# Weight loads of a fused delta-rule attention and MLP kernel, each split by partitions into two or four pieces

## The chip, the cores and the metric

The kernel runs on one core of a Trainium2 chip. A core has five engines that run side by side, each with a queue of its own that it works off in order: PE (TensorE: matmuls, and the weight loads before them, shown as PEld), DVE (VectorE), ACT (ScalarE), POOL (GpSimd) and SP (SyncE, which here only issues transfers). Transfers between the off-chip memory and the on-chip memory (SBUF, 128 partitions) are carried by 16 DMA engines. The metric is the time of the program in device microseconds (us), the median of several runs.

## The reference

For 4 batches and 8 heads a linear attention with the delta rule runs over 768 steps; its outputs, put side by side over the heads, give 3072 tokens of 384 numbers, which go through an MLP with 2048 hidden units.

```python
# q, k, v: (4, 8, 768, 48); beta: (4, 8, 768)
k_n = k / (np.linalg.norm(k, axis=-1, keepdims=True) + 1e-06)
for t in range(S):
    kt, vt, bt = (k_n[:, :, t].copy(), v[:, :, t].copy(), beta[:, :, t, None].copy())
    y[:, :, t] = np.einsum('bhd,bhde->bhe', q[:, :, t], state)
    v_old = np.einsum('bhde,bhd->bhe', state, kt)
    state = state + bt[:, :, :, None] * np.einsum('bhd,bhe->bhde', kt, vt - v_old)
# x: (3072, 384) from y; w_in: (384, 2048); w_out: (2048, 384)
h = x @ w_in
g = 0.5 * h * (1.0 + np.tanh(c * (h + 0.044715 * h * h * h)))
return g @ w_out
```

All inputs and the output are float32.

## The kernel before

**Tiling.** The 768 steps are cut into 12 chunks of 64 (`NC`), and each chunk into two units (`u = 2 * c + x`), each with half of the heads. For a unit, `prep` loads and normalizes k, turns k and q so that the head dimension lies on partitions (`kT`), takes the products of all pairs of steps (`G`, line 614), masks them (`ln`, `wp`) and inverts a triangular matrix by five rounds of doubling (operations `A` and `B`, line 684, with the block-diagonal tile `bd`). Then `chain` carries the state through the chunk: `K` and `R` (lines 729 and 742, where `R` subtracts from the scaled v), `U` (lines 755 and 765), `S` for the next state, `O` for the output. The output of a chunk is turned (`xT`) and fed to `mlp`: the up projection (`up`, line 842) with `W1`, the activation (`gelu`, line 847), the down projection (`down`, line 854) with `W2`, and the store of the rows. A chunk's MLP is 16 up blocks of three matmuls and, for each of two halves of its rows, 16 down matmuls in four operations of four.

**Weights.** `W1` is [128, 3, 2048] and `W2` is [128, 16, 384], both bf16 in SBUF, while `moe_w_in` and `moe_w_out` are float32 in memory: the transfer casts. Each is loaded in two halves by the function `weights` (lines 516 to 526), issued from POOL: the halves of `W1` by hidden units 0 to 1023 and 1024 to 2047, those of `W2` by the hidden blocks 0 to 7 and 8 to 15. Each load has 128 partitions. An up block waits for its half of `W1`, a down operation for its half of `W2`:

```python
A("pe", z + "up", up, reads=xn + [f"W1{0 if i < FC // 2 else 1}"], ...
A("pe", z + "down", down, reads=[f"{gn}.{f}" for f in range(i, i + 4)] + [f"{gn}s{i}", f"W2{0 if i < FC // 2 else 1}"], ...
```

**Order.** Every engine's order is written out by hand in the table `ORDER`, by names such as `w1.-3/0` (operation `w1` with position -3, first of its kind). `Flow.plans` works out the waits from what each operation reads and writes; several transfers that write the same buffer with the same semaphore (`dma=`) count it up together, and a reader waits for all of them. On POOL the four loads stand among other work: `w1.-3/0` between two `X1` selects (line 674), `w1.-2.9/0` between the halves of `R0` (line 734), `w2.-2/0` after `triw.1/0` (line 459) and before `binv.6/0` (line 550) and `vb.2.5/0` (line 739, the scaling of v that `R` waits for), and `w2.-1.9/0` between the `X1` selects of units 4 and 5. PE's queue begins with matmuls on zeros (`fill`, line 471) between the real work. PE's accumulators (PSUM) are given out by `BANKS` in PE's order, so a matmul can also wait for a bank that another engine has yet to read.

Of the kernel before, what the change touches and what calls it, by code (L numbers as in the profile page):

```python
# [122 lines left out]
    "pool": """  # L123
        masks.-12/0 masks.-12/2 bdz.4/0 half.-28/0 masks.-12/1 ident.-29/0 tmplz.-11/0 two.-12/0 ident2.-29/0 mlo.-12/0 two.-12/1
        bdz.7/0 mup.-12/0 mup.-12/1 mlo.-12/1 bdz.5/0 bneg.-28/0 X1h.0/0 X1h.0/1 binv.-140/0 X1h.1/1 kn.2/0 X1h.1/0 kn.3/0 X1.2/0
        X1.3/0 X1.2/1 w1.-3/0 X1.3/1 sq.6/0 binv.4/0 triw.-1/0 sq.8/0 R0.0.5/1 kn.4/0 w1.-2.9/0 R0.0.5/0 qb.4.01/0 pow.6/0 eps.6/0
        kn.5/0 triw.1/0 w2.-2/0 binv.6/0 vb.2.5/0 bdz.2/0 X1.4/1 X1.4/0 w2.-1.9/0 X1.5/0 X1.5/1 pow.8/0 kn.7/0 qb.6.01/0 eps.8/0
        qb.7.01/0 vb.4.5/0 kn.6/0 binv.8/0 kn.9/0 kn.8/0 bdz.3/0 qb.8.01/0 qb.9.01/0 pow.10/0 X1.6/0 eps.10/0 X1.6/1 X1.7/1 X1.7/0
        binv.10/0 X1.8/0 X1.8/1 X1.9/0 X1.9/1 kn.11/0 sq.12/0 vb.6.5/0 kn.10/0 qb.10.01/0 qb.11.01/0 bdc.8/1 bdc.8/0 pow.12/0
        bdc.9/1 X1.10/1 bdc.9/0 eps.12/0 X1.10/0 qb.13.01/0 binv.12/0 sq.14/0 X1.11/0 X1.11/1 qb.12.01/0 bdc.8/3 bdc.8/2 kn.13/0  # L130
# [215 lines left out]
def bass_deltanet__then__act_gelu_tanh_kernel(  # L346
# [10 lines left out]
    DM, FF = moe_w_in.shape  # L357
    assert (B, H, D) == (4, 8, 48) and DM == H * D and S % C == 0 and FF % 512 == 0
    NC, FC, J = S // C, FF // 128, DM // 128
# [4 lines left out]
    LIVE = {i: slice(0, C - 16) if i == 4 else slice(32, C) if i == 5 else slice(0, C) for i in range(1, 6)}  # L364
    UNIT = {4: slice(C - 16, C), 5: slice(0, 32)}

    F = Flow()
    A = F.add

    with nc.allow_non_contiguous_dma("strided loads"), nc.allow_low_precision("bf16 pipeline"):  # L370
        def sb(name, shape, dt=BF16, n=1):
            t = [nc.alloc_sbuf_tensor(f"{name}{i}", shape, dt).ap() for i in range(n)]
            return t if n > 1 else t[0]
# [17 lines left out]
        sq = sb("sq", [128, 2 * H, D], F32, 2)  # L391
# [19 lines left out]
        W1 = sb("W1", [128, J, FF])  # L411
        W2 = sb("W2", [128, FC, DM])
# [56 lines left out]
        def warm_up(n):  # L469
            def fill(e, P, i):  # L470
                return e.matmul(P(f"fill{i}")[:, :], wz[:, 0:128], wz[:, 0:512])  # L471
            for i in range(n):
                A("pe", "fill", lambda e, P, i=i: fill(e, P, i), reads=["wz"], alloc=(f"fill{i}", 1), frees=[f"fill{i}"], mode="m", pos=1e6, mm=1)
# [42 lines left out]
        def weights():  # L516
            w1v = moe_w_in.rearrange("(j p) f -> p j f", p=128)
            w2v = moe_w_out.rearrange("(n p) e -> p n e", p=128)
            for i in range(2):
                f0 = FF // 2 * i  # L520
                A("pool", "w1", lambda e, P, f0=f0: e.dma_start(W1[:, :, f0:f0 + FF // 2], w1v[:, :, f0:f0 + FF // 2]),
                  writes=[f"W1{i}"], dma=f"w1{i}", pos=-3 + 0.1 * i)
            for i in range(2):
                n0 = FC // 2 * i
                A("pool", "w2", lambda e, P, n0=n0: e.dma_start(W2[:, n0:n0 + FC // 2, :], w2v[:, n0:n0 + FC // 2, :]),
                  writes=[f"W2{i}"], dma=f"w2{i}", pos=-2 + 0.1 * i)

        def norms(c):
            z, r = "" if c else "0", c % NR
# [419 lines left out]
        for c in range(3):  # L949
            norms(c)  # L950
        weights()
        A("act", "tabG", lambda e, P: e.activation(one[:, :], one[:, :], ACT.Gelu_apprx_tanh),
          reads=["nrm00", "nrm01", "nrm10", "nrm20"], writes=["one"], pos=3)
# [17 lines left out]
        warm_up(ORDER["pe"].count("fill/"))  # L971
        F.schedule(ORDER, BANKS)
        G = Flow()
        banks = general(G)
        G.in_turn(banks)
        F.emit(nc, psum, G, flag[0:1, 0:1], flagged)

# [27 lines left out]
```

## Time and profile before

| | us |
|---|---|
| median of 3 runs (252.04 to 254.88) | 253.32 |
| the profiled execution | 252.5 |
| its span, first to last instruction | 250.8 |
| PE busy | 239.4 |
| DVE busy | 192.9 |
| ACT busy | 175.8 |
| POOL busy | 151.9 |

The profile shows one execution. Busy time is the time in which an engine ran something; an engine in order that waits for a semaphore holds up everything behind it in its queue. The granted clock is that of PE, as a share of full speed; over the whole span it was 0.993. The share of DMA is the mean busy share of the 16 DMA engines (it can exceed 1, because packets overlap), and GB/s is what they moved (counted in written bytes: the four weight loads together are 3.15 MB in the queue that carries them).

### The profile page before, as it was taken

To read this page: it belongs to the slowest core of one execution; us is meant where nothing else is said; L and a number is where in the kernel's file an instruction comes from. 1 tells how busy PE (TensorE), PEld (TensorE's weight loads), DVE (VectorE), ACT (ScalarE), POOL (GpSimd) and SP (SyncE) were. 2 spreads that over 40 slices of the span, in tenths; PEclk is the share of its full clock that TensorE was granted. 3 is DMA by queue.
4 is the path that set the end of the run, shared out by engine and by line. 5 is a ranking of instruction groups with operands and counts; after the bars stand their busy time and mean duration, and the time that the engine had idled before them with its cause. 6 is when DMAs were issued, how large, how long until landed. Compare 5 with 4: busy or idle time off the path is not lost.

```text
span 250.8 us, 11724 instructions
## 1 busy us (share of the span) xinstructions
PE 239.4 (95%) x5239; PEld 186.5 (74%) x5239; DVE 192.9 (77%) x330; ACT 175.8 (70%) x282; POOL 151.9 (61%) x229
## 2 busy tenths in 40 slices
PE   7799789799999998999999999999999999999996
PEld 3366577677877986888777898877887788886773
DVE  4999677859999997897898897998798688823110
ACT  5887569686998996886777786666775656663250
POOL 8268874894948667979858886877834444020000
PEclk9999979999999999999999999999999999999999
DMA  7989999974997997987898989948191241300124
GB/s 126 134 167 149 196 188 170 166 126 59 195 141 132 163 160 111 134 149 166 170 103 129 159 110 165 139 79 120 37 164 33 69 90 26 84 1 4 34 63 118
DMA packets 103367, 29.62 MB, mean 118 GB/s; under 512 B 96624, under 2 KB 102512, under 8 KB 103312
## 3 DMA queue, kind: packets, MB, share of 16 engines
q1 hardware_dynamic: 99248, 25.28, 64.5%
q0 software_dynamic: 2880, 3.15, 8.2%
q8 instruction: 43, 0.70, 1.2%
q10 hardware_dynamic: 1184, 0.39, 0.7%
q14 instruction: 12, 0.10, 0.1%
HBM read 20.55 MB, written 4.72 MB: 101 GB/s over the span
## 4 chain that ended last, share of the span: by engine, by line
PE 84%; DVE 5%; DMA 4%; issue 3%; ACT 2%; POOL 1%; ACTq 0%; POOLq 0%
PE ps L854 24%; PE ps L842 23%; PE ps L684 19%; PE ps L471 4%; PE ps L729 3%; PE ps L614 3%; PE ps L656 3%; DMA kT<-tok 2%; DMA xT<-xo 2%; PE ps L765 2%; PE ps L787 1%; PE ps L774 1%; PE ps L594 1%; ACT xi L418 1%; POOL vraw L739 1%
## 5 line engine op out<-in xcount | busy, mean ns | idle before, releaser
L842 PE MATMUL ps<-xT,W 128*128 128x256 bf16 x576 | 78.4, 273 | 0.4 <-DVE rs L742 0.2
L418 ACT ACTIVATE bd<-ps 64x512 bf16<-64x512 f32 x115 | 65.6, 588 | 14.6 <-PE ps L684 13.0
L854 PE MATMUL ps<-W,gT 128*128 128x384 bf16 x384 | 74.6, 326 | 0.0
L847 ACT ACTIVATE gT<-ps 128x1024 bf16<-128x1024 f32 x48 | 48.8, 1022 | 19.0 <-PE ps L842 18.4
L842 PEld LDWEIGHTS ps<-xT,W 128*128 128x128 bf16 x576 | 50.2, 98 | 7.4 <-DVE rs L742 0.4
L691 DVE TENSOR_TENSOR rt<-ps,two 128x512 bf16<-128x512 f32 x66 | 44.5, 685 | 9.9 <-PE ps L684 9.3
L678 POOL COPY bd<-xi 64x256 f32<-64x256 f32 x64 | 25.4, 403 | 34.3 <-ACT xi L418 26.3
L854 PEld LDWEIGHTS ps<-W,gT 128*128 128x128 bf16 x384 | 33.2, 98 | 16.1
L674 POOL TENSOR_SCALAR_AFFINE_SELECT bd<-ln 64x512 bf16<-64x512 bf16 x44 | 28.8, 657 | 18.2 <-DVE ln L635 14.0
L418 DVE CAST bd<-ps 64x512 bf16<-64x512 f32 x41 | 27.4, 680 | 3.9 <-PE ps L684 3.3
L691 DVE TENSOR_TENSOR rl<-ps,two 128x384 bf16<-128x384 f32 (+1 forms) x44 | 21.0, 483 | 12.1 <-PE ps L684 11.6
L418 ACT ACTIVATE xi<-ps 128x512 bf16<-128x512 f32 (+1 forms) x40 | 19.9, 509 | 12.8 <-PE ps L684 10.1
L544 POOL TENSOR_TENSOR nrm<-nrm,half 128x16 f32<-128x16 f32 x9 | 26.4, 2932 | 1.5 <-DVE nrm L541 1.3
L638 DVE CAST_PREDICATED wp<-mup,ps 128x1024 bf16<-128x1024 uint16 x22 | 26.6, 1214 | 0.2 <-PE ps L614 0.2
L684 PE MATMUL ps<-rt,bd 128*128 128x64 bf16 x528 | 25.6, 194 | 0.0
L684 PE MATMUL ps<-wp,bd 128*128 128x64 bf16 (+1 forms) x528 | 24.2, 188 | 1.3 <-issue 1.3
L684 PEld LDWEIGHTS ps<-rt,bd 128*128 128x128 bf16 x528 | 22.0, 98 | 4.0 <-DVE rt L691 0.4
L684 PEld LDWEIGHTS ps<-wp,bd 128*128 128x128 bf16 x528 | 21.4, 97 | 3.9 <-issue 1.4
L471 PE MATMUL ps<-wz 128*128 128x512 bf16 x61 | 18.9, 412 | 1.3 <-DVE wz L424 1.3
L571 POOL TENSOR_TENSOR tok<-kraw,nrm 128x384 bf16<-128x384 f32 x22 | 18.2, 833 | 2.1 <-PE ps L774 1.7
L418 ACT ACTIVATE xo<-ps 128x768 bf16<-128x768 f32 (+1 forms) x13 | 9.8, 760 | 10.1 <-PE ps L787 10.1
L684 PE MATMUL ps<-ln,bd 128*128 128x48 bf16 (+1 forms) x352 | 16.8, 190 | 0.0
(110 smaller groups left out, 333.1 us busy)
## 6 DMA issues: line engine op xcount, KB each, us to landing
vraw<-in_v_dram SPq DMA_DIRECT2D x24, 192.0 KB, 5.0
out_dram<-ob SPq DMA_DIRECT2D x47, 96.0 KB, 3.1
kraw<-in_k_dram SPq DMA_DIRECT2D x22, 192.0 KB, 5.1
qraw<-in_q_dram SPq DMA_DIRECT2D x18, 192.0 KB
W<-in_moe_w_in_dram POOLq DMA_DIRECT2D x2, 768.0 KB, 9.3
W<-in_moe_w_out_dram POOLq DMA_DIRECT2D x2, 768.0 KB, 9.9
qraw<-in_q_dram SPq DMA_DIRECT2D x12, 96.0 KB
kT<-tok SPq DMA_TRANSPOSE x18, 3.9
```

Source lines behind the costliest of these rows:

```text
L418: return e.activation(out, in_, ACT.Copy) if e is nc.scalar else e.tensor_copy(out, in_)
L471: return e.matmul(P(f"fill{i}")[:, :], wz[:, 0:128], wz[:, 0:512])
L544: e.tensor_tensor(nr[:, 1, hx], nr[:, 0, hx], half[:, hx], ALU.pow),
L571: A("dve" if u < 2 else POOL, z + "kn", lambda e, P: e.tensor_tensor(kn, kr, nr[:, 3, hx].rearrange("t (p g) -> t p g", p=2).unsqueeze(3). ...
L638: A("dve", z + "wp", lambda e, P: e.copy_predicated(wp[s][:, :, :], mup[:, :].bitcast(U16).unsqueeze(1).to_broadcast([128, H, 2 * C]), P(p ...
L674: A("pool", z + "X1", lambda e, P, src=src, dst=dst: e.affine_select(out=dst, in_=src, compare_op=ALU.not_equal, fill=-1.0, base=0, patter ...
L678: A("pool", z + "bdc", lambda e, P, src=src, dst=dst: e.tensor_copy(dst.bitcast(F32), src.bitcast(F32)), reads=[w("xi")], writes=[n(f"bd{a ...
L684: ins = e.matmul(P(name)[:, C * h + to.start:C * h + to.stop], bd[s][:, h, :], rhs[:, h, to])
L691: A("dve", z + f"rt{lo or str()}", lambda e, P, i=i, to=LIVE[i], r_=r_: e.tensor_tensor(r_[:, :, to], P(ps(f"A{i}")).rearrange("p (h t) -> ...
L842: ins = e.matmul(P(ph)[:, w * f:w * f + w].rearrange("p (x t) -> p x t", x=2), W1[:, j, 128 * (i + f):128 * (i + f) + 128], x_[:, :, j, :] ...
L847: A("act", z + "gelu", lambda e, P, i=i, ph=ph: e.activation(g_[:, i:i + nf, 0:w], P(ph).rearrange("p (f t) -> p f t", f=nf), ACT.Gelu_app ...
L854: ins = e.matmul(P(po)[:, 0:DM], g_[:, f, 128 * b:128 * b + 128], W2[:, f, :], start=(f == 0), stop=(f == FC - 1))
```

## The change

Each of the four loads becomes several transfers, each for a range of partitions: 120 and 8 for the first half of `W1`; 65, 49, 13 and 1 for its second half; 33, 33, 33 and 29 for the first half of `W2`; 120 and 8 for its second half. The pieces of a load are issued one right after another at the load's old place in POOL's order, count up the load's semaphore together, and their readers wait for all of them. Bytes, casts, places in memory, and the order of all other operations are the same.

```diff
     "pool": """
...
-        X1.3/0 X1.2/1 w1.-3/0 X1.3/1 sq.6/0 binv.4/0 triw.-1/0 sq.8/0 R0.0.5/1 kn.4/0 w1.-2.9/0 R0.0.5/0 qb.4.01/0 pow.6/0 eps.6/0
-        kn.5/0 triw.1/0 w2.-2/0 binv.6/0 vb.2.5/0 bdz.2/0 X1.4/1 X1.4/0 w2.-1.9/0 X1.5/0 X1.5/1 pow.8/0 kn.7/0 qb.6.01/0 eps.8/0
+        X1.3/0 X1.2/1 w1.-3/0 w1.-3/1 X1.3/1 sq.6/0 binv.4/0 triw.-1/0 sq.8/0 R0.0.5/1 kn.4/0 w1.-2.9/0 w1.-2.9/1 w1.-2.9/2 w1.-2.9/3 R0.0.5/0 qb.4.01/0 pow.6/0 eps.6/0
+        kn.5/0 triw.1/0 w2.-2/0 w2.-2/1 w2.-2/2 w2.-2/3 binv.6/0 vb.2.5/0 bdz.2/0 X1.4/1 X1.4/0 w2.-1.9/0 w2.-1.9/1 X1.5/0 X1.5/1 pow.8/0 kn.7/0 qb.6.01/0 eps.8/0
...
+    PARTS = [[(0, 120), (120, 128)], [(0, 65), (65, 114), (114, 127), (127, 128)], [(0, 33), (33, 66), (66, 99), (99, 128)], [(0, 120), (120, 128)]]
...
             for i in range(2):
                 f0 = FF // 2 * i
-                A("pool", "w1", lambda e, P, f0=f0: e.dma_start(W1[:, :, f0:f0 + FF // 2], w1v[:, :, f0:f0 + FF // 2]),
-                  writes=[f"W1{i}"], dma=f"w1{i}", pos=-3 + 0.1 * i)
+                for p0, p1 in PARTS[i]:
+                    A("pool", "w1", lambda e, P, f0=f0, p0=p0, p1=p1: e.dma_start(W1[p0:p1, :, f0:f0 + FF // 2], w1v[p0:p1, :, f0:f0 + FF // 2]),
+                      writes=[f"W1{i}"], dma=f"w1{i}", pos=-3 + 0.1 * i)
             for i in range(2):
                 n0 = FC // 2 * i
-                A("pool", "w2", lambda e, P, n0=n0: e.dma_start(W2[:, n0:n0 + FC // 2, :], w2v[:, n0:n0 + FC // 2, :]),
-                  writes=[f"W2{i}"], dma=f"w2{i}", pos=-2 + 0.1 * i)
+                for p0, p1 in PARTS[2 + i]:
+                    A("pool", "w2", lambda e, P, n0=n0, p0=p0, p1=p1: e.dma_start(W2[p0:p1, n0:n0 + FC // 2, :], w2v[p0:p1, n0:n0 + FC // 2, :]),
+                      writes=[f"W2{i}"], dma=f"w2{i}", pos=-2 + 0.1 * i)
```

## The prediction

> **What bounds the kernel now.** I read the page's totals first, then the chain that ended last, then the stretches in which the weights are loaded, then each engine's timeline there. The first lines are engine busy times, the chain by engine, and the queue that carries the weights (packets, MB, share of 16 engines); the last are stretches of the span with busy time of each engine, granted clock, DMA share and GB/s.
>
> ```profile
> span 250.8 us, 11724 instructions
> PE 239.4 (95%) x5239; PEld 186.5 (74%) x5239; DVE 192.9 (77%) x330; ACT 175.8 (70%) x282; POOL 151.9 (61%) x229
> ...
> q0 software_dynamic: 2880, 3.15, 8.2%
> ...
> PE 84%; DVE 5%; DMA 4%; issue 3%; ACT 2%; POOL 1%; ACTq 0%; POOLq 0%
> ...
> 30.00:32.00 2.00, 1.81 (x41) 1.45 (x40) 1.31 (x4) 0.90 (x2) 0.44 (x2) 0.82 1.29 153
> 32.00:35.00 3.00, 3.00 (x69) 2.46 (x65) 2.52 (x5) 2.17 (x7) 2.25 (x2) 0.55 1.15 201
> 35.00:38.00 3.00, 1.93 (x65) 1.61 (x61) 1.71 (x3) 1.77 (x4) 2.82 (x5) 1.00 1.07 170
> ...
> 49.00:53.00 4.00, 4.00 (x82) 3.50 (x79) 2.79 (x6) 3.77 (x7) 3.98 (x3) 1.00 1.26 195
> ...
> 60.00:251.00 191.00, 187.35 (x4124) 150.49 (x4121) 146.02 (x224) 131.19 (x195) 110.75 (x166) 1.00 0.68 108
> ```
>
> The reader is to see that PE carries the chain, and that after 60 us it is busy for 187.35 of 191 us. What PE loses before 60 us is therefore not made good later: there is no slack behind it. So the change is priced by what it makes PE wait for in the first 60 us. The weights move just there, while the DMA engines are full (shares of 1.07 to 1.29).
>
> **Who issues the weights, and when they are wanted.** The four loads are POOL instructions (durations in ns, first and last start; then time to landing), here with their neighbours in POOL's order:
>
> ```profile
> L521 POOL DMA_DIRECT2D W<-in_moe_w_in_dram x2: 807/915/1023, 21.7 to 28.6; - x2
> DMA to landing us min/median/max: 9.0/9.3/9.6
> L525 POOL DMA_DIRECT2D W<-in_moe_w_out_dram x2: 937/969/1001, 37.8 to 46.5; - x2
> DMA to landing us min/median/max: 8.5/9.9/11.3
> ...
> 22.71 0.68 POOL L674 TENSOR_SCALAR_AFFINE_SELECT bd<-ln 64x512 bf16<-64x512 bf16 x1
> ...
> 28.64 0.81 POOL L521 DMA_DIRECT2D W<-in_moe_w_in_dram  x1
> 29.47 0.84 POOL L734 TENSOR_TENSOR rs<-vraw,bsb 128x384 bf16<-128x384 f32 x1
> 31.87 0.50 POOL L418 CAST tok<-qraw 128x384 bf16<-128x384 f32 x1 [1.56 <-DMA qraw<-in_q_dram]
> 33.12 2.94 POOL L544 TENSOR_TENSOR nrm<-nrm,half 128x16 f32<-128x16 f32 x1 [0.74 <-DVE nrm L541]
> 36.15 0.27 POOL L546 TENSOR_SCALAR nrm<-nrm 128x16 f32<-128x16 f32 x1
> 36.51 0.83 POOL L571 TENSOR_TENSOR tok<-kraw,nrm 128x384 bf16<-128x384 f32 x1
> 37.28 0.61 POOL L459 COPY wp<-tmpl 128x512 f32<-128x512 f32 x1
> 37.84 1.00 POOL L525 DMA_DIRECT2D W<-in_moe_w_out_dram  x1
> 42.29 0.21 POOL L550 TENSOR_TENSOR nrm<-nrm,bsb 128x16 f32<-128x16 f32 x1 [3.46 <-DVE nrm L548]
> 42.47 1.46 POOL L739 TENSOR_TENSOR vraw<-vraw,bsb 128x768 f32<-128x768 f32 x1
> ...
> 46.46 0.94 POOL L525 DMA_DIRECT2D W<-in_moe_w_out_dram  x1
> 47.41 1.47 POOL L674 TENSOR_SCALAR_AFFINE_SELECT bd<-ln 64x512 bf16<-64x512 bf16 x2
> ...
> 59.72 0.22 POOL L550 TENSOR_TENSOR nrm<-nrm,bsb 128x16 f32<-128x16 f32 x1 [3.35 <-DVE nrm L548]
> ```
>
> Their users, and PE's waits among them (brackets: idle before, and its cause):
>
> ```profile
> 25.16 0.40 PE L684 MATMUL ps<-wp,bd 128*128 128x64 bf16 x8
> 30.19 0.22 PE L614 MATMUL ps<-kT 48*64 48x64 bf16 x3 [1.44 <-issue]
> 35.65 0.24 PE L755 MATMUL ps<-rs,xi 64*64 64x48 bf16 x4
> 36.96 0.62 PE L755 MATMUL ps<-rs,xi 64*64 64x48 bf16 x28 [1.07 <-issue]
> 40.37 0.38 PE L580 MATMUL ps<-ident,tok 128*128 128x128 bf16 x4
> 43.97 0.96 DVE L742 TENSOR_TENSOR rs<-ps,vraw 128x768 bf16<-128x768 f32 x1 [0.90 <-POOL vraw L739]
> 44.99 1.16 PE L842 MATMUL ps<-xT,W 128*128 128x256 bf16 x9 [0.24 <-DVE rs L742]
> 48.62 0.29 PE L684 MATMUL ps<-wp,bd 128*128 128x64 bf16 x4 [1.28 <-issue]
> 50.72 0.60 PE L684 MATMUL ps<-wp,bd 128*128 128x32 bf16 x16
> 51.95 0.81 PE L854 MATMUL ps<-W,gT 128*128 128x384 bf16 x4
> 54.72 0.22 PE L729 MATMUL ps<-st,kT 48*64 48x48 bf16 x4 [0.50 <-issue]
> 58.02 1.46 PE L854 MATMUL ps<-W,gT 128*128 128x384 bf16 x8
> ```
>
> Landing minus wanted: the second half of W1 lands at about 28.64 + 9.0 to 9.6 = 38 and is first read at 44.99 (the third block of up projections): 7 us to spare. The first half of W2 lands at 37.84 + 11.3 = 49.1 and is read at 51.95: under 3 us. The second half of W2 lands at 46.46 + 8.5 = 55.0 and is read at 58.02: 3 us. No wait for W stands in the trace; the covers are thin.
>
> **The change, term by term.**
>
> *Eight more issues on POOL.* Each piece costs one issue: 0.92 us (L521) or 0.97 us (L525). W2 has 2.7 times the rows of W1 (1024 against 384) and costs 6% more, so I take a piece as dear as a whole load; the low end is nothing, the high end 1.02 us. Behind the waiting POOL stand these, one after another. The first load's extra issue moves the select at 22.71 to end at 24.3, before PE's 25.16. The second load's three put the L734 product at 33.2 to 34.0; PE wants it at 35.65. The cast at 31.87 moves to 34.0, where POOL's waits of 1.56 and 0.74 us cover most of it. The power at 33.12 goes to 34.5, the L571 product ends at 38.7 (wanted at 40.37), and the third load begins at 39.2. Its four issues end at 43.1, the fourth beginning at 42.1. The L550 product at 42.29 had a wait of 3.46 us, so it moves only by 0.8, and so does the L739 product at 42.47, which DVE was already waiting for (0.90) and PE behind DVE (0.24). That is the place where POOL reaches PE: **0.8 us**. The fourth load's extra issue moves the selects at 47.41 to end near 50.6; their user stands in the group at 50.72, itself 0.8 later, and waits for nothing. The wait of 3.35 us at 59.72 swallows the rest.
>
> *How the rows are spread over the engines.* This is the dear unknown. The loads of before have 128 partitions, and every other transfer in the code 32, 64 or 128; no row shows 120, 8, 65, 49, 13, 1, 33 or 29. In the stretch from 49 to 53 us, nearly all weights, 195 GB/s are written, 12.2 GB/s for each of 16 engines. The half of W2 (0.786 MB) takes 4.0 us at that rate, so 8.5 - 4.0 = 4.5 us of the landing time is start and completion. A piece of 29 partitions holds 29 x 8 x 384 x 2 B = 178 kB. Spread over about 16 engines it takes 0.9 us, below the lag; on one engine 178 kB / 12.2 GB/s = 14.6 us. The nearest row, the 128-partition load, speaks for the even end. But 128 is 16 equal shares of 8, and 29 has no equal shares except one of 29 (33 has 11 of 3, 65 has 13 of 5, 49 has 7 of 7, 120 has 15 of 8). If equal shares are the rule behind that row, only the 29 is ruinous. I take the one-engine end as somewhat likelier, and keep both for the range.
>
> With it the first half of W2 is whole at 42.1 + 4.5 + 14.6 = 61.2, and PE wants it at 51.95 + 0.8 = 52.75: a stall of **8.5 us** at the first down projection. Every later PE operation is queued behind it; ACT, DVE and POOL run dry within a few us. Late next is the second half of W2: on that engine its share, 52 kB, is 4.3 us more, whole at 65.5; wanted 58.02 - 51.95 = 6.1 after PE resumes, at 67.3. No second stall.
>
> *The clock.* After PE's 1.44 us wait before 30.19 the granted clock was 0.82 and 0.55 in the stretches from 30 to 35 us: (1 - 0.82) x 2 + (1 - 0.55) x 3 = **1.7 us** of PE lost. I charge the same once behind an 8.5 us stall; the low end is nothing, since the other waits of over 1 us, at 36.96 and 48.62, lost no clock that the stretches show.
>
> *W1 in uneven shares* costs nothing: stacked on one engine the shares are 5 + 7 + 1 + 1 = 14 partitions against 8, at most 4.0 x 6/8 = 3.0 us more at the rate above; from the issue of the 49 at 30.5 the half is whole by 30.5 + 9.6 + 3.0 = 43.1, wanted at 45.8.
>
> Sum: 0.8 + 8.5 + 1.7 = 11.0 us. The profiled execution took 252.5 us (span 250.8), so 263.5; the runs' median of 253.3 is 0.8 above it, which makes **264**.
>
> The Trainium skill, in "DMA: Bandwidth & Descriptors", section "Why a DMA increments its semaphore by 16 and not by 1", states that a transfer uses the largest number of engines up to 16 that divides its outermost size on both sides, with 127 partitions on one engine as an example. By that the 29 gets one engine, as in the sum. The same section names a measured exception for some direct copies from GpSimd, which get the partitions divided by 16, rounded up, on each engine. By that the 29 spreads over 15 engines at two each, and the time is the first rival's. The trace has no such piece and cannot choose.
>
> **The rivals.**
>
> *Spread anyway, no change to measure.* If uneven pieces share out at ceil(partitions/16) each, the fullest engine holds 3 + 3 + 3 + 2 = 11 partitions of the third load instead of 8: 4.0 x 11/8 = 5.5 us, and the whole has landed at 39.2 + 4.5 + 5.5 = 49.2, or 3 us later if the 11.3 us of the slower W2 load is the measure. PE wants it at 52.75. Only the 0.8 us stays: 253.3 on the profiled scale, 254 for the median. For it: the nearest row. Against it: the shares have to be uneven.
>
> *Faster.* PE's four waits marked "issue" lie inside one instruction group, where no semaphore can be the cause, and each falls while weights move: 1.44 + 1.07 + 1.28 + 0.50 = 4.3 us; the lost clock is 1.7 more. I read them as PE's instructions arriving late behind weight rows. If pieces leave some engines free (13 of 16, 11 of 16, 8 of 16) these arrive in time, and it decides once W2's first half still lands before 52.75: 252.5 + 0.8 - 6.0 = 247.3 if all vanish, 250 if half do. Against it: the same bytes move for longer in the same busy stretch, and the waits can as well grow.
>
> *POOL pays more.* Up to 0.97 us an issue only 0.8 reaches PE, since POOL's waits are used up there; beyond, ten issues (seven of them added) stand ahead of the L739 product, so each 0.1 us more costs 1.0. At 1.3 us an issue: 0.8 + 10 x 0.35 = 4.3, or 257. Against it: W2's rows cost POOL next to nothing.
>
> **How the numbers follow.** One engine for the 29: 0.50, own range 258 to 269 (no clock loss and cheaper issues below; a second lost clock stretch, or loads of q, k and v held up behind the full engine, above). Spread: 0.25, of which 0.15 within 1%, 0.06 slower, 0.04 faster. Faster: 0.13. POOL dearer: 0.12, slower. One per cent, 2.5 us, is about what a measurement of this kernel can tell from no change. Faster 0.04 + 0.13 = 0.17; same 0.15; slower 0.50 + 0.06 + 0.12 = 0.68. The range of 250 to 270 leaves out most of the faster case and a tail above, under 0.2.
>
> **What would show it.** Right: twelve issues of W with about 0.95 us each; an idle of PE before an L854 group near 53 us that ends on a DMA of W, 6 to 10 us long; a landing time near 19 us for the 29-partition piece against under 10 for the others; a stretch behind it at a clock near 0.5; the span after that stall as long as before. Wrong: no wait of PE for W (then the pieces spread); POOL's issues well off 0.95; or the "issue" waits of PE gone.

## The result and the profile after

The changed kernel takes 270.08 us (269.03 to 271.17), the one before 254.1 us beside it: a ratio of 1.0636, with an interval of 1.0568 to 1.0703. The forecast was 264, with a range of 250 to 270, and the time lies just above that range: the way and the place of the stall were right, its length was not. A ratio is taken over the fast executions of both kernels (those within 1.5% of the kernel's fastest), so it can differ from the ratio of two medians. The profiled execution of the changed kernel took 271.17 us. From its page: totals, the queue of the weights, the chain of waits by engine and by line.

```profile
span 269.4 us, 11732 instructions
PE 243.5 (90%) x5239; PEld 189.0 (70%) x5239; DVE 192.8 (72%) x330; ACT 175.5 (65%) x282; POOL 158.0 (59%) x237
...
q0 software_dynamic: 7280, 3.16, 9.9%
...
PE 73%; DMA 14%; POOL 7%; DVE 3%; issue 1%; ACT 1%; POOLq 0%
PE ps L858 23%; PE ps L846 20%; PE ps L688 16%; DMA W<-in_moe_w_out_dram 10%; PE ps L473 4%; PE ps L733 3%; PE ps L618 2%; DMA kT<-tok 2%; DMA xT<-xo 2%; PE ps L769 2%; PE ps L791 1%; POOL W L524 1%; POOL nrm L548 1%; POOL sq L544 1%; DVE rt L665 1%
```

PE's busy time grows by 4.1 us (243.5 against 239.4), the span by 18.6 us: PE stands still for most of the difference. A transfer of W2 now stands in the chain with 10%, and the weights' queue has 7280 packets instead of 2880 for the same bytes. (Line numbers are higher by up to 4: 842 is now 846, 854 is 858.)

The weight issues of the changed kernel by line (durations in ns, first and last start, then times to landing), and below them the piece of 29 in the list of transfers (KB, us to landing):

```profile
L524 POOL DMA_DIRECT2D W<-in_moe_w_in_dram x6: 584/684/1057, 22.1 to 31.8; - x6
L529 POOL DMA_DIRECT2D W<-in_moe_w_out_dram x6: 581/753/1937, 38.4 to 49.6; - x6
DMA to landing us min/median/max: 6.5/9.3/27.0
```

```profile
W<-in_moe_w_out_dram POOLq DMA_DIRECT2D x1, 174.0 KB, 27.0
```

A piece costs POOL 0.6 to 0.75 us as a rule, and one of them 1.94; the longest landing, 27.0 us, is that of the 29. POOL's timeline around the third load, and PE's up to the next chunk's first up block:

```profile
38.44 4.07 POOL L529 DMA_DIRECT2D W<-in_moe_w_out_dram  x4
44.49 0.22 POOL L554 TENSOR_TENSOR nrm<-nrm,bsb 128x16 f32<-128x16 f32 x1 [1.97 <-DVE nrm L552]
44.67 1.47 POOL L743 TENSOR_TENSOR vraw<-vraw,bsb 128x768 f32<-128x768 f32 x1
```

```profile
30.93 0.22 PE L618 MATMUL ps<-kT 48*64 48x64 bf16 x3 [2.06 <-issue]
37.85 0.94 PE L759 MATMUL ps<-rs,xi 64*64 64x48 bf16 x28 [2.44 <-issue]
47.25 1.16 PE L846 MATMUL ps<-xT,W 128*128 128x256 bf16 x9
51.69 0.29 PE L688 MATMUL ps<-wp,bd 128*128 128x64 bf16 x4 [2.09 <-issue]
54.78 0.40 PE L688 MATMUL ps<-rl,bd 128*128 128x64 bf16 x8
67.65 1.46 PE L858 MATMUL ps<-W,gT 128*128 128x384 bf16 x4 [12.47 <-DMA W<-in_moe_w_out_dram]
78.59 2.13 PE L846 MATMUL ps<-xT,W 128*128 128x256 bf16 x18
```

The four issues of the third load take 4.07 us in all, and the operation behind them at 44.49 still waits for DVE, not for POOL. PE's first, second and fourth row are its waits inside a group, which stood at 1.44, 1.07 and 1.28 before; the sixth row is the new wait. The up block at 47.25, which had waited for DVE and POOL, waits no more.

Stretches of the span (busy time of PE, PEld, DVE, ACT, POOL, then clock, DMA share, GB/s):

```profile
36.00:40.00 4.00, 2.15 (x49) 1.74 (x52) 0.77 (x2) 1.34 (x3) 3.82 (x7) 0.59 1.13 140
40.00:43.00 3.00, 3.00 (x75) 2.67 (x66) 2.96 (x5) 2.26 (x5) 2.51 (x2) 0.50 1.19 141
43.00:47.00 4.00, 4.00 (x115) 3.06 (x113) 2.74 (x6) 3.41 (x6) 2.51 (x3) 0.93 1.50 154
...
62.00:67.00 5.00, 0.00 (x0) 0.00 (x0) 0.00 (x0) 0.00 (x0) 0.00 (x0) 0.50 0.09 12
67.00:70.00 3.00, 2.35 (x15) 1.34 (x16) 0.42 (x1) 0.42 (x1) 0.00 (x0) 0.50 0.05 6
70.00:77.00 7.00, 7.00 (x183) 5.06 (x181) 4.62 (x8) 3.71 (x6) 0.63 (x2) 0.94 0.11 22
```

The row from 62 to 67 us is the change in one line: every engine of the core stands still, the DMA engines are busy for 0.09 x 16 = 1.4 engines' worth (packets overlap on one engine), and 12 GB/s arrive. That is near the 12.2 GB/s that the prediction worked out for one engine. The whole kernel waits for the one engine that carries the piece of 29.

**Where the 18.6 us went**, by PE's timeline in both profiles. PE reaches the first down projection at 67.65 - 12.47 = 55.18 instead of 51.95: +3.2. It waits there: +12.5. From there to the first up block of the next chunk it takes 10.9 instead of 10.1 us: +0.9. From that block to the end it takes 190.8 instead of 188.8: +2.0. The sum is 18.6. The first two belong together: what frees PE at 67.65 is the landing of the 29, 27.0 us after its issue at 40.58, so the 3.2 us that PE lost on its way there only shorten its wait.

### The profile page after: what moved, and what is told of

It is laid out like the page before. It is cut to its first block, busy times and chain, and to the rows that moved or that the text cites. A ratio compares the mean times of both kernels' runs of the same rounds, so it can differ in the third digit from the quotient of the medians.

```text
span 269.4 us, 11732 instructions
## 1 busy us (share of the span) xinstructions
PE 243.5 (90%) x5239; PEld 189.0 (70%) x5239; DVE 192.8 (72%) x330; ACT 175.5 (65%) x282; POOL 158.0 (59%) x237
## 3 DMA queue, kind: packets, MB, share of 16 engines
q0 software_dynamic: 7280, 3.16, 9.9%
## 4 chain that ended last, share of the span: by engine, by line
PE 73%; DMA 14%; POOL 7%; DVE 3%; issue 1%; ACT 1%; POOLq 0%
PE ps L858 23%; PE ps L846 20%; PE ps L688 16%; DMA W<-in_moe_w_out_dram 10%; PE ps L473 4%; PE ps L733 3%; PE ps L618 2%; DMA kT<-tok 2%; DMA xT<-xo 2%; PE ps L769 2%; PE ps L791 1%; POOL W L524 1%; POOL nrm L548 1%; POOL sq L544 1%; DVE rt L665 1%
## 5 line engine op out<-in xcount | busy, mean ns | idle before, releaser
L858 PE MATMUL ps<-W,gT 128*128 128x384 bf16 x384 | 75.9, 330 | 12.5 <-DMA W<-in_moe_w_out_dram 12.5
L851 ACT ACTIVATE gT<-ps 128x1024 bf16<-128x1024 f32 x48 | 48.8, 1022 | 19.2 <-PE ps L846 18.6
L682 POOL COPY bd<-xi 64x256 f32<-64x256 f32 x64 | 25.5, 404 | 34.5 <-ACT xi L420 26.3
L420 DVE CAST bd<-ps 64x512 bf16<-64x512 f32 x41 | 27.5, 681 | 19.3 <-PE ps L688 18.7
L688 PE MATMUL ps<-rt,bd 128*128 128x64 bf16 x528 | 26.3, 195 | 0.0
L688 PEld LDWEIGHTS ps<-rt,bd 128*128 128x128 bf16 x528 | 22.8, 100 | 4.1 <-issue 0.6
L473 PE MATMUL ps<-wz 128*128 128x512 bf16 x61 | 21.1, 452 | 1.4 <-DVE wz L426 1.3
```

Source lines behind the costliest of these rows:

```text
L420: return e.activation(out, in_, ACT.Copy) if e is nc.scalar else e.tensor_copy(out, in_)
L682: A("pool", z + "bdc", lambda e, P, src=src, dst=dst: e.tensor_copy(dst.bitcast(F32), src.bitcast(F32)), reads=[w("xi")], writes=[n(f"bd{a ...
L688: ins = e.matmul(P(name)[:, C * h + to.start:C * h + to.stop], bd[s][:, h, :], rhs[:, h, to])
L851: A("act", z + "gelu", lambda e, P, i=i, ph=ph: e.activation(g_[:, i:i + nf, 0:w], P(ph).rearrange("p (f t) -> p f t", f=nf), ACT.Gelu_app ...
L858: ins = e.matmul(P(po)[:, 0:DM], g_[:, f, 128 * b:128 * b + 128], W2[:, f, :], start=(f == 0), stop=(f == FC - 1))
```

## The experiments

All edits are to the list of parts in the changed kernel; the number of issues in POOL's order follows it. Medians, and ratios to the kernel before with their intervals.

**The piece of 29, taken away and left alone.** The first two runs undo the split of the third load, and do it alone.

```diff
# third load whole
-    [(0, 33), (33, 66), (66, 99), (99, 128)]
+    [(0, 128)]
# only the third load split: the other three become
+    [(0, 128)]
```

> The first half of W2 is one 128-partition load again; the other three loads stay split as in the change. Theory A (the 29-partition piece runs on one DMA engine, 232 rows at 12 a us, and PE waits for it): no wait of PE for W, and what is left is what the other pieces cost, longer waits marked issue before 55 us: 254 to 258 us. Theory B (every extra piece costs, through POOL's issue and the rows it adds, whatever its size): five of the eight extra pieces are left, so five eighths of the 16 us: about 264.

Measured: 257.86 us, 1.0223 (1.0171 to 1.0275). PE does not wait for W. Some 4.7 us above the kernel before (253.19 beside it) are left. The profiled execution was the shortest of the four (254.88), so its profile shows a part of them at most. In it PE has a wait that the kernel before did not have:

```profile
34.53 1.04 PE L598 MATMUL ps<-ident,tok 128*128 128x128 bf16 x8 [1.70 <-POOL tok L420]
```

It waits for POOL's cast of q, which ran from 33.97 to 34.47, with only one product between it and the four issues of W1's second half. The run without a prime, below, has the same wait with 1.78 us, the one with the 29 first with 0.90.

> Only the first half of W2 is split, 33+33+33+29; the other three are whole. Theory A: PE waits some 13 us at the first down projection, the piece of 29 lands about 27 us after its issue; 266 to 269 us. Theory B: three of eight extra pieces, about 260.

Measured: 267.1 us, 1.0569 (1.0528 to 1.0609). PE's row in this kernel, and its pieces of W2 in the list of transfers:

```profile
64.63 1.46 PE L858 MATMUL ps<-W,gT 128*128 128x384 bf16 x4 [14.03 <-DMA W<-in_moe_w_out_dram]
```

```profile
W<-in_moe_w_out_dram POOLq DMA_DIRECT2D x1, 768.0 KB, 23.5
W<-in_moe_w_out_dram POOLq DMA_DIRECT2D x3, 198.0 KB, 6.9
W<-in_moe_w_out_dram POOLq DMA_DIRECT2D x1, 174.0 KB, 25.0
```

So the split of one load of four makes 5.7 of the 6.4 per cent. The 2.2 per cent of the other three loads do not add to it: PE comes to the first down projection at 50.60 here and at 55.18 in the change, and in both it goes on only when the load has landed. The last W2 load, whole again here, also takes 23.5 us to land, where it took 8.5 before: its share on the full engine stands behind the 29 in the same queue, as the prediction had it.

**Is it the pieces, or their partition counts?** As many pieces in the same places, but with other counts:

```diff
# sixteens
+    [(0, 112), (112, 128)], [(0, 64), (64, 96), (96, 112), (112, 128)], [(0, 32), (32, 64), (64, 96), (96, 128)], [(0, 112), (112, 128)]
# no prime: only the third load differs from the change
-    [(0, 33), (33, 66), (66, 99), (99, 128)]
+    [(0, 33), (33, 66), (66, 98), (98, 128)]
```

> As many pieces as in the change, at the same places, but all multiples of 16: 112+16, 64+32+16+16, 32+32+32+32, 112+16. Theory A: every piece uses 16 engines, 2816 rows and 12 x 16 four-byte packets (3008 in all in the weights' queue), no wait for W, 253 to 256 us. Theory B: as the change, 270.

Measured: 255.04 us, 1.013 (1.0045 to 1.0214), no wait for W, 3008 packets.

> As the change, but the first half of W2 in 33+33+32+30, so 11, 11, 16 and 15 engines and none on one. Theory A: no wait for W, 254 to 258 us, near the run with the third load whole. Theory B, or a cost of four late pieces whatever their counts: 268 to 270.

Measured: 255.62 us, 1.0117 (1.0038 to 1.0195), no wait for W. One partition moved from the third piece to the last, 33 to 32 and 29 to 30, takes away some 13 to 14 us. Theory B is out: twelve issues at the same places cost about 1%.

**How much, by rows on the fullest engine.** Two more sizes of the piece on one engine, with only the third load split:

```diff
# 75+53
+    [(0, 75), (75, 128)]
# 17+96+15
+    [(0, 17), (17, 113), (113, 128)]
```

> Only the first half of W2 is split, 75+53. Theory A (largest divisor up to 16; the fullest engine's rows set the landing): 75 goes to 15 engines, 40 rows each, 53 to one, 424 rows; that engine has 464 rows against 280 with 33+33+33+29, 184 more at 12 a us, 15 us later: 280 to 285 us. Packets in the weights' queue: 2816 rows + 5 x 16 + 40 + 15 x 424 = 9296. Rival (a piece costs by being late and uneven, not by its rows on one engine): about 263 to 267, as there are fewer pieces than with 33+33+33+29.

Measured: 278.0 us, 1.0968 (1.0853 to 1.1082; two runs), 9296 packets to the packet.

> Only the first half of W2 is split, 17+96+15: 17 on one engine (136 rows), 96 on 16, 15 on 15; the fullest engine has up to 192 rows, against 280 with 33+33+33+29 and 464 with 75+53. From those two, 10.4 us for 184 rows: whole 22 us after its first issue, PE waits about 9 us, 260 to 264 us. Packets 2816 + 6 x 16 + 15 x 136 + 8 = 4960. Rival (the cost is one of any piece on one engine, whatever its rows): 267.

Measured: 258.72 us, 1.0198 (1.0118 to 1.0278), 4960 packets. PE's waits for W and the issues of W2 by line, first in 75+53, then in 17+96+15:

```profile
L529 POOL DMA_DIRECT2D W<-in_moe_w_out_dram x3: 901/981/3113, 36.8 to 45.4; - x3
```

```profile
74.47 1.44 PE L858 MATMUL ps<-W,gT 128*128 128x384 bf16 x4 [23.22 <-DMA W<-in_moe_w_out_dram]
```

```profile
L529 POOL DMA_DIRECT2D W<-in_moe_w_out_dram x4: 612/876/1473, 36.6 to 43.6; - x4
```

```profile
48.39 0.29 PE L688 MATMUL ps<-wp,bd 128*128 128x64 bf16 x4 [3.46 <-issue]
55.48 0.89 PE L858 MATMUL ps<-W,gT 128*128 128x384 bf16 x4 [2.06 <-DMA W<-in_moe_w_out_dram]
```

From the load's first issue to PE's start the three profiles give 18.9 us (17+96+15, up to 192 rows on the fullest engine), 27.2 (33+33+33+29 alone, about 280) and 37.6 (75+53, 464). The cost grows with the rows on that engine and not with the number of pieces. Both runs came out some us below what I expected. For 17+96+15 the wait of 9 us was 2.1: I had laid a straight line through two points, and the smaller one falls below it; PE also came 1.5 us later there, after a wait marked issue of 3.46. For 75+53 the packet records of the trace give the reason. (They do not name the engine; all the loads' even shares had been carried by then, so the rows that are left are those of the 53.) From 58 to 63 us the engine carries 12 rows of W and 12 of the other loads in each us, one for one; from 65 to 74 the other loads are through, and it carries 16 to 17 rows of W. In the changed kernel the engine shares one for one to the end (12 and 12 in each us from 63 to 67, strictly in turn).

**Order within the load.**

```diff
-    [(0, 33), (33, 66), (66, 99), (99, 128)]
+    [(99, 128), (0, 33), (33, 66), (66, 99)]
```

> As the change, but in the third load the piece of 29 is issued first and the three of 33 behind it. Theory A1 (the fullest engine has 232 + about 48 rows in whatever order): the load is whole within 3 us of before, at 65 to 68 us, 267 to 270 us. Theory A2 (the 29 was late because it was issued last, with 7 us from its issue to its first rows): whole at 60 to 62, PE waits 6 us less, 263 to 265 us.

Measured: 270.53 us, 1.0691 (1.0615 to 1.0766). PE starts the first down projection at 66.16, after a wait of 10.49, 27.4 us after the load's first issue against 29.2 in the change. Theory A1 holds: the engine has its rows to carry in any order. (The landing times of pieces that share a semaphore can't be told apart when a long one goes first, so PE's start is used here.)

**A piece of 29 with a deadline far off.** 29 partitions in the first half of W1, all else whole:

```diff
+    [(0, 99), (99, 128)], [(0, 128)], [(0, 128)], [(0, 128)]
```

> A piece of 29 again, but in the first half of W1 (99+29), which is issued 20 us before it is wanted; the other loads whole. Theory A: one engine has 29 x 3 + 9 x 3 = 114 rows of W1 and the load lands some 20 us after its issue at 21.7, just where it is wanted: PE waits 0 to 3 us, 253 to 258 us. Packets in the weights' queue 2816 + 5 x 16 + 5 x 27 + 15 x 87 = 4336. Rival (the piece of 29 costs by holding up the other queues on its engine, wherever it stands): 13 us as in the third load, 266.

Measured: 262.34 us, 1.0381 (1.0337 to 1.0425), slower than I expected of theory A. The wait for W is as foreseen, 3.07 us. But another follows, here on PE, POOL, DVE and SP's queue (start, duration, wait before):

```profile
44.02 0.82 PE L846 MATMUL ps<-xT,W 128*128 128x256 bf16 x3 [3.07 <-DMA W<-in_moe_w_in_dram]
...
53.94 2.10 PE L846 MATMUL ps<-xT,W 128*128 128x256 bf16 x9 [4.79 <-DVE rs L746]
```

```profile
37.24 10.17 SPq L515 DMA_DIRECT2D vraw<-in_v_dram  x1
```

```profile
51.41 1.47 POOL L743 TENSOR_TENSOR vraw<-vraw,bsb 128x768 f32<-128x768 f32 x1 [9.14 <-DMA vraw<-in_v_dram]
```

```profile
52.92 0.96 DVE L746 TENSOR_TENSOR rs<-ps,vraw 128x768 bf16<-128x768 f32 x1 [10.08 <-POOL vraw L743]
```

SP takes 10.17 us to issue this load of v, where such an issue took 1.04 at 37.11 before; POOL waits 9.14 us for it, DVE for POOL, PE for DVE. The packet records fit one crowded engine: from 40 to 45 us 5 to 6 rows of W1 go each us, one by one in turn with as many rows of SP's loads, and in the us from 48, when W1's last rows go, 699 rows of SP's loads. By this the share of v on that engine comes late. The rival of this run was right in kind: here a piece with time to spare held up the other queues on its engine. In the changed kernel no such wait shows: there PE already stands still for W2.

**What the harmless splits cost.** Three runs without any piece on one engine: W1 alone split as in the change; all loads 120+8; all loads 32+32+32+32 with the pieces set apart in POOL's order.

```diff
# W1 only
+    [(0, 120), (120, 128)], [(0, 65), (65, 114), (114, 127), (127, 128)], [(0, 128)], [(0, 128)]
# all 120+8
+    four times [(0, 120), (120, 128)]
# spread: four times [(0, 32), (32, 64), (64, 96), (96, 128)], and in POOL's order
+    kn.3/0 w1.-3/0 w1.-3/1 X1.2/0 X1.3/0 X1.2/1 w1.-3/2 w1.-3/3 ... triw.-1/0 w1.-2.9/0 w1.-2.9/1 ... kn.4/0 w1.-2.9/2 w1.-2.9/3
+    qb.4.01/0 w2.-2/0 pow.6/0 w2.-2/1 ... kn.5/0 w2.-2/2 triw.1/0 w2.-2/3 binv.6/0 w2.-1.9/0 ... bdz.2/0 w2.-1.9/1 ... X1.4/0 w2.-1.9/2 w2.-1.9/3
```

> Only the two halves of W1 are split (120+8, 65+49+13+1), W2 is loaded whole. It prices what is left when the 29 is gone. If the pieces of W1 hold up PE's instructions longer: waits marked issue before 40 us grow from 2.5 to about 4 us and the time is 255 to 258. If they cost nothing: 252 to 254.

Measured: 256.29 us, 1.0041 (0.9993 to 1.0089): no cost that stands out, but the ten runs lie between 253.45 and 258.70. In the profiled one (256.92) PE comes to the first down projection 3.0 us later than before, about as late as in the change:

```profile
54.96 0.81 PE L858 MATMUL ps<-W,gT 128*128 128x384 bf16 x4
```

> All four loads in 120+8: 15 engines with 8 partitions each and 8 engines with one. The fullest engine holds 9 partitions against 8, four extra issues of some 0.6 us. If uneven pieces as such cost: 255 to 258. If only few engines cost: 252 to 255. If a spare engine lets PE's instructions through (the faster rival of the prediction): under 251.

Measured: 253.62 us, 0.9939 (0.9892 to 0.9986). At most a gain of 1%, not the 2 to 3% of the faster rival.

> All four loads in 32+32+32+32, and the pieces not one behind another but set apart in POOL's order, from before the first X1 select to behind X1.4, at most two together. If the bursts of weight rows are what holds up PE's instructions, the waits marked issue before 60 us fall from 4.3 us to half and the time is 249 to 252; if not, 252 to 256.

Measured: 253.53 us, 1.0051 (0.9991 to 1.0111). The waits marked issue did not go away when the bursts did. These two are left before 60 us:

```profile
25.18 0.22 PE L660 MATMUL ps<-rt,xi 64*64 64x64 bf16 x2 [2.01 <-issue]
33.39 0.22 PE L618 MATMUL ps<-kT 48*64 48x64 bf16 x3 [2.98 <-issue]
```

They come to 5.0 us instead of 4.3, fewer and longer. So the weights coming in bursts is not what makes them.

The packet records show what PE waits for there. In all thirteen kernels every wait of PE marked issue of 0.4 us or more ends 1.3 to 1.9 us behind the end of a 16 KB packet of the instruction queue, q8. In the kernel before such packets end at 28.72, 35.60, 47.09 and 53.32 us, and the four waits at 30.19, 36.96, 48.62 and 54.72. By this PE waits for its own instructions. Why some of these packets come too late is open: a wait of 0.74 us at 96.92 in the kernel before falls long after its last weights have landed.

## Why the prediction was right or wrong

**The spread of the rows: right, and now shown.** The prediction had argued one engine for the 29 from equal shares and held it at 0.50. The counts of packets settle it. A load of before has 16 semaphore packets; the four have 2816 rows + 64 = 2880. If each piece runs on the largest number k of engines up to 16 that divides its partitions (for the piece of one partition, its three rows: k = 3), and every engine gets as many packets as the fullest one, the empty places being filled with packets of 4 B, then the change has 2816 rows, 12 x 16 semaphore packets, and 24 + 24 + 45 + 189 + 9 + 13 + 3 x 120 + 3480 + 64 + 64 = 4272 fillers, 3480 of them for the 29: 7280. The queue's row says 7280. The same sum gives the measured 3392, 3008, 3696, 6768, 3248, 3296, 9296, 4336, 4960 and 3072 of the other kernels, without a difference of one. That is the rule of the Trainium skill, "DMA: Bandwidth & Descriptors", section "Why a DMA increments its semaphore by 16 and not by 1". Its exception for some direct copies from GpSimd, partitions over 16 rounded up, did not apply to any of these casting loads.

**The stall: right in place, 8.5 foreseen and 12.5 measured.** The step that failed is the term of 4.5 + 14.6 = 19.1 us from the issue of the 29 to its landing; it was 27.0. The engine's rate was right: alone it carried 16 to 17 rows of 768 B a us in the 75+53 run, 12.3 to 13.1 GB/s, against the 12.2 reckoned. What was left out is that W does not have this rate to itself. The other loads take every other row: 12 rows of 768 B a us are 9.2 GB/s, so 178 kB take 19.3 us, not 14.6. The prediction named loads held up behind the full engine as a reason for its upper end, but not that they slow the 29. The other 3 us of the 27.0 no run takes apart; rows of the three 33s on the same engine (24 of each that falls on it) and an issue of 1.94 us instead of 0.97 stand for them. The run with the 29 first shows that their order changes little. Against that the fourth issue began at 40.58, 1.5 us earlier than reckoned, and PE came at 55.18, 2.4 us later than the 52.75 reckoned: 8.5 + 7.9 - 1.5 - 2.4 = 12.5.

**No second stall at W2's second half: right.** Its smaller piece landed 19.5 us after its issue at 49.6, so at 69.1; the first block that reads it began at 74.59 without a wait.

```profile
W<-in_moe_w_out_dram POOLq DMA_DIRECT2D x1, 48.0 KB, 19.5
```

The 52 kB reckoned for its share on the full engine are neither of the two possible shares (8 partitions of 6144 B are 49 kB, 9 are 55); nothing hangs on it. That W1's uneven shares cost no wait for W was right too.

**POOL's 0.8 us: wrong.** POOL paid less than I said (busy 158.0 against 151.9, so 6.1 us for eight issues, not 7.5) and kept a wait of 1.97 us at 44.49; its product at 44.67 was there in time, since PE itself came later. The place was wrong too. The prediction moved the cast of q to 34.0, ending at 34.5, and did not ask who reads it, a group of PE that in the kernel before began at 33.97:

```profile
33.97 0.94 PE L594 MATMUL ps<-ident,tok 128*128 128x128 bf16 x8
```

In the profiles with the third load whole, without a prime and with the 29 first PE waits just there, 1.70, 1.78 and 0.90 us. In the change the cast ended at 33.74 and PE's group began at 33.80.

What PE did lose before the stall, 3.2 us, has another cause, which the prediction had only as a rival's reverse ("the waits can as well grow"): the three waits marked issue at 30.93, 37.85 and 51.69 went from 1.44 + 1.07 + 1.28 = 3.8 to 6.6 us. The clock stayed low from 36 to 47 us, which by the rows above is at most 0.41 x 4 + 0.5 x 3 + 0.07 x 4 = 3.4 us of PE instead of 1.7 (at most, since PE stood still for part of it). None of this moved the end, since PE then waits for the landing. Whether the pieces make these waits longer is not shown: PE comes to the first down projection at 54.96 in the profile of W1's pieces alone, but at 52.1 to 52.7 in those with the third load whole, without a prime and with sixteens, which split W1 too (51.95 before). Where these last three kernels lose their 1.2 to 2.2% is shown only in part, by the wait for the cast.

**The clock after the stall: right.** PE was busy for 2.35 us at half the clock and then for 7 us at 0.94: 0.5 x 2.35 + 0.06 x 7 = 1.6 us against the 1.7 charged. The down projections behind the stall took 0.9 us more in all, since a wait of 0.50 us in them was gone.

**The end.** The prediction let the rest run as before. It took 2.0 us more. In the profiles of the kernels with the third load whole, without a prime and with sixteens the stretch from the first down projection to the end is 200.5 to 201.8 us, against 198.9 before and 201.8 after: it is longer without the 29 too, and the profile of before lies at the low end of its kind. Why is open.

In the prediction's own terms: 0.8 + 8.5 + 1.7 = 11.0 us became 3.2 + 12.5 + 0.9 + 2.0 = 18.6. The landing was 6.4 us later than reckoned (67.6 instead of 61.2), the clock cost 0.8 less behind it, and 2.0 came at the end.

**The rivals.** Spreading anyway is refuted by the packet counts. The faster one is refuted by the all-120+8 run, where some engines have no share in a piece and the waits marked issue still come to 4.4 us (2.26 + 0.26 + 0.36 + 1.48). That POOL pays more for an issue holds only for long pieces: 1.47 us for 136 rows on one engine, 1.94 for 232, 3.11 for 424, which is 5 to 6 ns a row.

## What to carry to other kernels

Cut a transfer by partitions only into counts with a large divisor up to 16; the cost of a piece is the rows on its fullest engine, and a prime count above 16 puts all of it on one. Price such an engine with what else runs on it, for here it shared row for row with the other queues, and look at both sides: who waits for the piece, and whose loads have a share on that engine. Count a queue's packets before and after: here they told the spread to the last packet before any time was explained.

## What the hardware showed that was not expected

Engines without a share in a piece still get packets, 4 B each, until all have as many as the fullest: 3480 for the piece of 29, 6360 for the 53. PE's waits inside a group of matmuls end 1.3 to 1.9 us behind a 16 KB packet of the instruction queue, in all thirteen kernels. Two queues with work on one engine took turns row by row, 768 B or 2048 B of one and 192 B of the other. The POOL instruction that issues a piece grows with the rows of the fullest engine (the three durations above), which the loads of before, with 24 and 64 rows on each engine, did not show.
